# A spectral mixer and an ELU feed-forward layer on one core: the opening's second table as a sum of two short series, other queue orders and PSUM tiles

## The chip, the cores and the metric

The kernel runs on one core of a Trainium2 chip. The core has a matrix engine (TensorE, PE in the profile, its weight loads PEld), a vector engine (VectorE, DVE), a scalar engine (ScalarE, ACT), a general engine (GpSimd, POOL), a queue engine for transfers (SyncE, SP) and 16 DMA engines. Every engine works through its own instructions in order and waits on the others by semaphores. The metric is the device time of one execution in microseconds (us), as a median of several runs.

## The reference

```python
X = np.fft.rfft(x, axis=1)                      # x: (8, 3008, 256)
Xr, Xi = X.real, X.imag
Yr = Xr @ w_r - Xi @ w_i + b_r                  # w_r, w_i: 256 x 256
Yi = Xr @ w_i + Xi @ w_r + b_i
Yr = np.sign(Yr) * np.maximum(np.abs(Yr) - 0.01, 0.0)
Yi = np.sign(Yi) * np.maximum(np.abs(Yi) - 0.01, 0.0)
y = np.fft.irfft(Yr + 1j * Yi, n=3008, axis=1)
h = y.reshape(24064, 256) @ w_in                # w_in: 256 x 2048
g = np.where(h > 0, h, np.exp(np.minimum(h, 0)) - 1)
return g @ w_out                                # w_out: 2048 x 256
```

## The kernel before

The transform over 3008 = 47 x 64 points is done as matmuls with tables of sines: stage A along the 64 (table M1, six units of four rows each), stage X along the 47 with twiddle factors (table M2, eight units), stage M with the weight matrices and the soft threshold (six pairs of groups), stage B back along the 64 (table M3, six units), stage Y back along the 47 (table M4). Between A and X, and between B and Y, the data change their layout by a trip through DRAM: A is stored to DA and read back as Z, B is stored to DB and read back as Bs. The feed-forward layer takes blocks of 512 tokens and pairs of 128 hidden columns: `front` (L790) multiplies by w_in and takes the exponential, `elu` and `finish_elu` make gT, `back` (L848) multiplies by w_out.

The order on every engine is that of the program text (`manual_schedule`, L86). After the opening a plan mixes the units of the next batch between the pairs. In the opening nothing of the feed-forward runs: batch 0 goes through A, X, M, B and the first two units of Y alone, and the first `front` comes behind them. All that the change touches lies in this opening.

The tables are not inputs; they are computed. GpSimd writes integers with iotas (L405), VectorE makes angles of them, ACT takes the sine. M2 has 32 slots (s) of 2 x 48 columns on 96 partitions and is made in four quarters of eight slots: `points` (L498: integer product modulo 64, an index kv, its half as a sign st), `phases` (L514: index times a factor of the partition, plus a phase, on VectorE or ACT), `wraps` (L529: subtract the nearest integer), `sizes` (L541: absolute value, ACT), `signs` (L535) and `sines` (L545: ACT, into M2). `slot0` (L551) masks slot 0. The third table is v3 (L629), its remainder w3 (L676, L677), its absolute value a3 (L683), and two sines (L690), then two products into M3 (L694, L698).

Transfers of x run on GpSimd's queue (L118), in six pieces of 512 KB for batch 0 (`first_x`) and three of 1 MB for batch 1 (`load_x`), the latter behind `gate` (L664), a copy of one column of Z that keeps GpSimd until that part of Z has landed. Stores of A (L157), loads of the weights w_r, w_i (L588, L589), Z (L166), bias rows (L372, L597), w_in (L648), stores of B (L262) and loads of Bs (L273) run on SyncE's queue. GpSimd turns the weights into the bf16 matrices wcat_r and wcat_s (L590 to L593).

`m_group` (L187) does one group of M: four matmuls of 512 columns, with one more in front for the bias if `biased` (L191: a matrix of ones times bias_p, whose rows 0, 32 and 64 hold three bf16 parts of the bias). `first_M` (L222) calls it biased or not in turn; without, VectorE adds bias_bc (L204). The parts are made by L678 to L687.

`idle_pe(n)` (L363) issues n matmuls of 512 columns whose result nobody reads. PSUM in the opening is three pools: pre2 (two tiles of two banks, used by A, X, B and Y), pre1 (three of one bank, for M) and pre0 (the idle matmuls). `unit_X` (L168) does eight matmuls into one pre2 tile and `evac` (L125) copies it to XT on VectorE (L127) or ACT (L129); units 1, 4 and 7 on VectorE.

## Time and profile before

| | us |
|---|---|
| median of 3 runs (lowest to highest) | 910.41 (909.49 to 911.92) |
| the profiled execution | 909.7 |
| its span | 907.9 |
| PE busy in the span | 885.0 (97%) |
| DVE, ACT, POOL busy | 721.0, 698.9, 313.0 |
| first matmul of A, of X, of M | 5.86, 22.43, 30.03 |
| first matmul of B, of the feed-forward | 35.39, 54.07 |

Span is the time from the first to the last instruction of the profile. The page says for each engine how long it was busy; the chain of waits follows the work that ended last back to the start. A granted clock of 1.00 means that TensorE ran unthrottled. One stretch of the opening, with busy time and number of instructions of PE, PEld, DVE, ACT and POOL, then granted clock, DMA share (the mean busy share of the 16 engines) and GB/s:

```profile
22.40:30.70 8.30, 5.47 (x73) 3.60 (x72) 7.53 (x10) 5.45 (x8) 5.45 (x7) 1.00 1.05 321
```

Costs of single operations in the opening, from the trace: a VectorE tensor_scalar of 96x384 f32 0.35, tensor_tensor 0.55, scalar_tensor_tensor 0.61; an ACT activation of 96x384 0.51; an evacuation of X 0.80 on ACT and 0.96 on VectorE; an evacuation of A 1.01 on ACT; a DMA issue on SyncE about 0.25 to 0.54 and on GpSimd 0.6 to 0.8.

### The profile page before, as it was taken

The numbers are of one execution on the slowest core, as the hardware profiler recorded it, in microseconds if no ns is written. First come the engines' busy times: TensorE is split into PE (matmuls) and PEld (weight loads), VectorE is DVE, ScalarE is ACT, GpSimd is POOL, SyncE is SP. The second block draws the span as 40 slices with busy tenths as digits, with TensorE's granted clock in tenths as the row PEclk, the third lists the DMA queues.
The fourth block names the chain that finished last, engine by engine and source line by source line (L and its number), as shares of the span: only waits on it lengthen the run. The fifth ranks groups of instructions, "written<-read, shape, count | busy, mean of one in ns | idle before, by whom it ended". The sixth has DMA issues, their size and how long they took to land.

```text
span 907.9 us, 17273 instructions
## 1 busy us (share of the span) xinstructions
PE 885.0 (97%) x6665; PEld 653.1 (72%) x6768; DVE 721.0 (79%) x901; ACT 698.9 (77%) x855; POOL 313.0 (34%) x436
## 2 busy tenths in 40 slices
PE   9879999999999999999999999999999999999997
PEld 3457667876678676876678766787667866777775
DVE  8779778887788778887788877888778877778776
ACT  6678778787878788788787888878787877777664
POOL 7700440233331431405404153133332134443664
PEclk9999999999999999999999999999999999999999
DMA  8997025721383215722176031752228111221011
GB/s 270 310 258 233 24 70 174 222 70 48 93 232 117 70 48 155 199 88 93 53 204 186 25 106 58 205 167 80 61 73 229 32 40 47 84 80 48 24 47 47
DMA packets 90623, 106.06 MB, mean 117 GB/s; under 512 B 5270, under 2 KB 81308, under 8 KB 87180
## 3 DMA queue, kind: packets, MB, share of 16 engines
q1 hardware_dynamic: 84284, 77.42, 30.5%
q0 software_dynamic: 5968, 27.26, 9.1%
q8 instruction: 53, 0.87, 0.4%
q10 hardware_dynamic: 288, 0.26, 0.1%
q14 instruction: 30, 0.25, 0.1%
HBM read 55.12 MB, written 49.81 MB: 116 GB/s over the span
## 4 chain that ended last, share of the span: by engine, by line
PE 84%; DVE 5%; ACT 4%; DMA 3%; issue 2%; POOL 0%; SPq 0%; DVEq 0%; ACTq 0%; POOLq 0%
PE ps_o L848 34%; PE hps L790 33%; PE mps L194 9%; PE yps L347 2%; PE bps L246 2%; PE aps L146 2%; PE xps L177 2%; DVE gT L817 1%; ACT Bz L259 1%; ACT Et L804 1%; DMA Bs<-DB 1%; DVE Et L829 1%; DMA Z<-DA 1%; ACT Et L801 1%; DMA DB<-Bz 1%
## 5 line engine op out<-in xcount | busy, mean ns | idle before, releaser
L848 PE MATMUL ps_o<-w_out_r,gT 128*128 128x256 f32 x3008 | 476.9, 301 | 0.2 <-DVE gT L815 0.2
L848 PEld LDWEIGHTS ps_o<-w_out_r,gT 128*128 128x128 f32 x3008 | 403.6, 189 | 49.9 <-DVE osb L859 1.3
L790 PE MATMUL hps<-yT,w_in_s 128*128 128x512 bf16 (+7 forms) x1651 | 382.3, 351 | 6.6 <-ACT Bz L259 1.1
L815 DVE SCALAR_TENSOR_TENSOR gT<-Et,hps 128x512 fp32r<-128x512 f32 (+1 forms) x268 | 220.3, 850 | 74.1 <-POOL Et L827 37.6
L817 DVE SCALAR_TENSOR_TENSOR gT<-hps,Et 128x1024 fp32r<-128x1024 f32 x200 | 244.6, 1223 | 16.2 <-DVE Et L829 0.5
L790 PEld LDWEIGHTS <-w_in_s 128*128 128x128 bf16 x1728 | 141.6, 98 | 129.7 <-issue 22.7
L804 ACT ACTIVATE Et<-hps 128x1024 f32<-128x1024 f32 x200 | 206.1, 1030 | 11.1 <-PE hps L790 4.4
L827 POOL TENSOR_SCALAR Et<-Et 128x512 f32<-128x512 f32 x183 | 109.2, 615 | 219.4 <-ACT Et L799 219.4
L829 DVE TENSOR_SCALAR Et<-Et 128x1024 f32<-128x1024 f32 x200 | 138.6, 693 | 48.0 <-ACT Et L804 39.9
L212 POOL TENSOR_SCALAR clip<-yb 128x512 f32<-128x512 f32 x84 | 51.8, 616 | 318.1 <-DVE yb L204 286.0
L799 ACT ACTIVATE Et<-hps 128x512 f32<-128x512 f32 x184 | 99.9, 595 | 62.8 <-PE hps L790 62.1
L801 ACT ACTIVATE Et<-hps 128x1024 f32<-128x1024 f32 x84 | 86.2, 1027 | 71.8 <-PE hps L790 70.2
L213 POOL TENSOR_TENSOR Y<-yb,clip 128x512 bf16<-128x512 f32 x84 | 107.3, 1277 | 7.0
L802 ACT ACTIVATE Et<-Et 128x1024 f32<-128x1024 f32 x84 | 88.9, 1058 | 2.7
L204 DVE TENSOR_TENSOR yb<-mps,bias_bc 128x512 f32<-128x512 f32 x89 | 61.3, 689 | 35.5 <-PE mps L194 23.2
L129 ACT CAST XT<-xps 128x768 bf16<-128x768 f32 x61 | 48.8, 799 | 15.4 <-PE xps L177 15.4
L129 ACT CAST yT<-yps 128x752 bf16<-128x752 f32 (+1 forms) x64 | 49.8, 779 | 13.4 <-PE yps L347 13.2
L129 ACT CAST A<-aps 128x1024 bf16<-128x1024 f32 (+1 forms) x47 | 47.2, 1004 | 13.2 <-PE aps L146 11.6
L194 PE MATMUL mps<-wcat_r,XT 128*128 128x512 bf16 x180 | 55.6, 384 | 0.8 <-ACT Bz L259 0.3
L194 PE MATMUL mps<-wcat_s,XT 128*128 128x512 bf16 x182 | 54.9, 379 | 0.7
L194 PEld LDWEIGHTS <-XT 128*128 128x128 bf16 x384 | 30.8, 98 | 29.6 <-DVE XT L127 0.6
L259 ACT CAST Bz<-bps 128x1024 bf16<-128x1024 f32 x46 | 46.1, 1001 | 2.8 <-PE bps L246 2.8
(121 smaller groups left out, 414.3 us busy)
## 6 DMA issues: line engine op xcount, KB each, us to landing
xt<-in_x_dram POOLq DMA_DIRECT2D x21, 1024.0 KB, 7.5
out_dram<-osb SPq DMA_DIRECT2D x158, 128.0 KB
Bs<-DB SPq DMA_DIRECT2D x31, 384.0 KB
DA<-A SPq DMA_DIRECT2D x21, 512.0 KB
DB<-Bz SPq DMA_DIRECT2D x21, 512.0 KB
Z<-DA SPq DMA_DIRECT2D x7, 1152.0 KB
Z<-DA SPq DMA_DIRECT2D x11, 384.0 KB
xt<-in_x_dram POOLq DMA_DIRECT2D x6, 512.0 KB, 5.8
```

Source lines behind the costliest of these rows:

```text
L129: nc.scalar.copy(dst, src)
L194: nc.tensor.matmul(ps, lhsT=XT[:, dt, c, o : o + P], rhs=wm[:, dt, :], start=(not biased and m == 0 and dt == 0), stop=(m == 1 and dt == 1),)
L213: nc.gpsimd.tensor_tensor(Y_of[b, q][:, i, :], yb, clip[:], ALU.subtract)
L790: nc.tensor.matmul(hps[:, s, c0:c1], lhsT=w_in_s[:, dt, ft * P : ft * P + P], rhs=yT_of[b][:, dt, t0 : t0 + c1 - c0], start=(dt == 0), sto ...
L799: nc.scalar.activation(E_[:, s], hps[:, s], AF.Exp)
L801: nc.scalar.activation(E_, hps[:], AF.Relu, scale=-1.0)
L804: nc.scalar.activation(E_, hps[:], AF.Exp)
L815: nc.vector.scalar_tensor_tensor(o, e, -1.0, h, ALU.add, ALU.max)
L817: nc.vector.scalar_tensor_tensor(o, h, 0.0, e, ALU.max, ALU.add)
L827: eng.tensor_scalar(E_[:, s], E_[:, s], 1.0, 0.0, ALU.min, ALU.max)
L829: nc.vector.tensor_scalar(E_, E_, 1.0, -1.0, ALU.min, ALU.add)
L848: nc.tensor.matmul(po[q][:, i_ % 2, :], lhsT=gT[:, s, i_ * P : i_ * P + P], rhs=w_out_r[:, ft, :], start=(ft == 0 and i_ % 2 == 0), stop=( ...
```

## The change

The index of M2's angle is a product modulo the length; the new text writes the angle as a sum of a term in s alone (`sp`, 32 columns) and a term that depends on a difference only (`tab`, 78 columns), of which `window` takes overlapping, also reversed, pieces without copying; `tsg` holds the sign in the same form. `short_tables` makes them, `sums` adds them in two halves of 16 slots, `wraps` is one instruction that also turns the sign, which the sine's scale takes back. Two columns (n47, sp32) are added; the integer arrays mi, kv, st, r2 and their iotas are dropped.

The first piece of x is loaded ahead of all iotas; ten idle matmuls instead of nine stand at the start and 30 instead of 40 before X. The sixth unit of A is evacuated in halves, one on ACT and one on VectorE, with a store each. On SyncE's queue the loads of Z come ahead of w_r and w_i. The bias is loaded as 8 rows of 64, split into parts on VectorE (`split_bias`), stored to DRAM (bias_d) and loaded back into rows 0, 32 and 64 of bias_p, which GpSimd clears. In X there are three PSUM tiles of two banks, VectorE evacuates units 1, 2, 4, 5 and 7, the third table's work is moved ahead of and into X, and wcat_r, wcat_s are made behind it by VectorE, ACT and GpSimd. The pools pre2 and pre1 are opened behind X. The four matmuls of the first M group are ordered by dt first. The gate of batch 1's loads reads slot 24 of Z.

```diff
-    pre2 = first.enter_context(tc.tile_pool(name="pre2", bufs=2, space=bass.MemoryType.PSUM))
-    pre1 = first.enter_context(tc.tile_pool(name="pre1", bufs=3, space=bass.MemoryType.PSUM))
     pre0 = first.enter_context(tc.tile_pool(name="pre0", bufs=1, space=bass.MemoryType.PSUM))
+    sooner = ExitStack()
+    pre2 = sooner.enter_context(tc.tile_pool(name="preX", bufs=3, space=bass.MemoryType.PSUM))
...
+        j0 = 8 * ci
+        if alone and u == 5:
+            for j in range(2):
+                c = 4 * uu + 2 * j
+                evac(A[:, c : c + 2, :].rearrange("p n d -> p (n d)"), ps[:, j, :], bool(j))
+                nc.sync.dma_start(dav[:, j0 + c : j0 + c + 2, :], A[:, c : c + 2, :])
+            return
...
-        for m, (c, wm) in enumerate(((0, wcat_r), (1, wcat_s))):
-            for dt in range(2):
-                nc.tensor.matmul(
-                    ps, lhsT=XT[:, dt, c, o : o + P], rhs=wm[:, dt, :],
-                    start=(not biased and m == 0 and dt == 0), stop=(m == 1 and dt == 1),
-                )
+        for n_ in range(4):
+            c, dt = (n_ % 2, n_ // 2) if (b, q, i) == (0, 3, 0) else (n_ // 2, n_ % 2)
+            nc.tensor.matmul(
+                ps, lhsT=XT[:, dt, c, o : o + P], rhs=(wcat_r, wcat_s)[c][:, dt, :],
+                start=(not biased and n_ == 0), stop=n_ == 3,
+            )
...
-    brow, rest = (wk3.tile([P, 2 * D], F32, name="yb", tag="yb") for _ in range(2))
-    nc.vector.memset(brow[:], 0.0)
-    for o, bv in ((0, b_r), (D, b_i)):
-        for k in range(3):
...
-    idle_pe(9)
+    BR, BC = 8, 2 * D // 8
+    brow, rest = (wk3.tile([BR, BC], F32, name="yb", tag="yb") for _ in range(2))
+    bpart = wk3.tile([BR, 3, BC], BF16, name="yb", tag="yb")
+    bias_d = dram.tile([3, BR, BC], BF16, name="bias_d", tag="bias_d")
     xts = []
...
+    def first_x(u):
+        load_x(0, u // 2, 4 * (u % 2), 4 * (u % 2) + 4)
+    first_x(0)
+    idle_pe(10)
+    def split_bias():
+        nc.vector.tensor_copy(bpart[:, 0], brow[:])
+        nc.vector.tensor_tensor(rest[:], brow[:], bpart[:, 0], ALU.subtract)
+        nc.vector.tensor_copy(bpart[:, 1], rest[:])
+        nc.vector.tensor_tensor(rest[:], rest[:], bpart[:, 1], ALU.subtract)
+        nc.vector.tensor_copy(bpart[:, 2], rest[:])
...
+        w_r_f = stagep.tile([P, 2, D], F32, name="w_r_f")
+        w_i_f = stagep.tile([P, 2, D], F32, name="w_i_f")
+        for o, bv in ((0, b_r), (BR // 2, b_i)):
+            nc.sync.dma_start(
+                brow[o : o + BR // 2, :],
+                bass.AP(tensor=bv.tensor, offset=bv.offset, ap=[[BC, BR // 2], [1, BC]]),
+            )
...
-        first_x(0)
         first_x(1)
-        mi = stagep.tile([P, NS, K1, 2], I32, name="mi")
-        kk1 = row("kk1", [P, K1, 2])
-        iota("", None, [[1, K1]], out=kk1[:, :, 0])
-        iota("", None, [[-1, K1]], out=kk1[:, :, 1])
         first_x(2)
-        for s0, s1 in ((0, 8), (8, NS)):
...
-                first_x(4)
+        TD, TL = N2 - NS // 2 + K1 // 4, N2 + K1 // 2 + 2
+        trow = iota("trow", [P, TL], [[1, TL]], base=-TD)
+        tji = stagep.tile([P, TL], I32, name="tji")
+        iota("", None, [[-15, TL]], base=15 * TD + 6 * N2, out=tji[:])
+        first_x(3)
+        first_x(4)
+        first_x(5)
+        nc.gpsimd.memset(bias_p[:], 0.0)
...
+        n47 = mix(dve, n1c, 4.0 / N1, qd, ALU.mult, ALU.mult)
+        sp32 = mix(dve, n1s, float(NS), qd, ALU.mult, ALU.add)
...
+        tab = row("tab", [P, TL])
+        tmp = row("tmp", [P, TL])
+        tsg = row("tsg", [P, TL])
+        sp = row("sp", [P, NS])
+        z = slice(0, RZ)
+        def window(t, s0, ns, c, b):
+            return bass.AP(
+                tensor=t.tensor, offset=t[0:RZ, TD - s0 : TD - s0 + 1].offset,
+                ap=[t[0:RZ].ap[0], [-1, ns], [1 - 2 * c, K1]],
+            )
+        def short_tables():
+            dve.tensor_scalar(tmp[:], trow, 36.0 / N1, CMAGIC, ALU.mult, ALU.add)
+            dve.tensor_scalar(tmp[:], tmp[:], -CMAGIC, -float(N1), ALU.add, ALU.mult)
+            dve.scalar_tensor_tensor(tmp[:], trow, 36.0, tmp[:], ALU.mult, ALU.add)
+            dve.tensor_scalar(tmp[:], tmp[:], n47[:], None, ALU.mult)
+            dve.tensor_scalar(tab[:], tmp[:], CMAGIC, -CMAGIC, ALU.add, ALU.add)
+            dve.tensor_tensor(tab[:], tmp[:], tab[:], ALU.subtract)
+            dve.tensor_scalar(sp[:], srow[:, 0:NS], n1s[:], ph[:], ALU.mult, ALU.add)
+            dve.tensor_scalar(tji[:], tji[:], N2 - 1, None, ALU.bitwise_and)
+            dve.tensor_scalar(tsg[:], tji[:], NS + 0.5, -0.5, ALU.is_gt, ALU.add)
+        def kt(t, s0, s1):
+            return t[z, s0:s1].rearrange("p s (k t) -> p s k t", t=2)
+        def sums(s0, s1):
+            for c in range(2):
+                dve.tensor_tensor(
+                    kt(v2, s0, s1)[:, :, :, c],
+                    sp[z, s0:s1].unsqueeze(2).to_broadcast([RZ, s1 - s0, K1]),
+                    window(tab, s0, s1 - s0, c, None), ALU.add,
+                )
+            if s0 == 0:
+                dve.tensor_scalar(
+                    kt(v2, 0, 1)[:, 0, :, 1], tab[z, TD - NS : TD - NS + K1], sp32[z], None,
+                    ALU.add,
+                )
+        def wraps(s0, s1):
+            v = v2[z, s0:s1]
+            dve.scalar_tensor_tensor(v, v, 0.5, v, ALU.is_gt, ALU.subtract)
+        def sizes(s0, s1):
+            nc.scalar.activation(a2[z, s0:s1], v2[z, s0:s1], AF.Abs)
+        def signs(s0, s1):
+            for c in range(2):
+                a = kt(a2, s0, s1)[:, :, :, c]
                 dve.scalar_tensor_tensor(
-                    kv[z, 0, :, 1], mi[z, 0, :, 1], float(N1), kk1[z, :, 0], ALU.mult, ALU.add
+                    a, a, qd[z], window(tsg, s0, s1 - s0, c, None), ALU.subtract, ALU.mult
                 )
-            kf = k_.rearrange("p s k t -> p s (k t)")
...
-        def wraps(g):
-            gs, z = slice(8 * g, 8 * g + 8), slice(0, RZ)
-            v, r = v2[z, gs], r2[z]
-            dve.tensor_scalar(r, v, CMAGIC, -CMAGIC, ALU.add, ALU.add)
-            dve.tensor_tensor(v, v, r, ALU.subtract)
...
+        def sines(s0, s1, c):
             nc.scalar.activation(
-                M2[:, gs, c, :], (v2, a2)[c][z, gs], AF.Sin, bias=0.0, scale=TURN * (1.0 + c)
+                M2[:, s0:s1, c, :], (v2, a2)[c][z, s0:s1], AF.Sin, bias=0.0,
+                scale=(-TURN, 2.0 * TURN)[c],
             )
...
-            unit_A(0, u, alone=True)
+            unit_A(0, u, alone=True, on_dve=False)
...
-        points(0)
-        phases(0)
-        wraps(0)
-        for u in range(4):
+        short_tables()
+        sums(0, 16)
+        wraps(0, 16)
+        sums(16, 32)
+        wraps(16, 32)
+        for u in range(6):
             fA(u)
-        points(1)
-        phases(1, True)
-        points(2)
-        sizes(0)
-        fA(4)
-        wraps(1)
-        signs(0)
-        fA(5)
+            if u == 2:
+                sizes(0, 16)
+                signs(0, 16)
+        for g in range(4):
+            load_Z(0, 8 * g, 8 * g + 8)
         nc.sync.dma_start(w_r_f[:], w_r.rearrange("(c p) e -> p c e", p=P))
         nc.sync.dma_start(w_i_f[:], w_i.rearrange("(c p) e -> p c e", p=P))
-        pool.tensor_copy(wcat_r[:, :, 0:D], w_r_f[:])
-        pool.tensor_copy(wcat_r[:, :, D : 2 * D], w_i_f[:])
-        pool.tensor_scalar(wcat_s[:, :, 0:D], w_i_f[:], -1.0, None, ALU.mult)
-        pool.tensor_copy(wcat_s[:, :, D : 2 * D], w_r_f[:])
-        for g in range(4):
-            load_Z(0, 8 * g, 8 * g + 8)
+        sizes(16, 32)
+        signs(16, 32)
+        sines(0, 16, 0)
+        sines(0, 16, 1)
+        slot0()
+        sines(16, 32, 0)
+        sines(16, 32, 1)
+        split_bias()
+        nc.sync.dma_start(bias_d.rearrange("k r c -> r k c"), bpart[:])
         for o, bv in ((0, b_r), (D, b_i)):
             nc.sync.dma_start(
                 bias_bc[:, o : o + D],
                 bass.AP(tensor=bv.tensor, offset=bv.offset, ap=[[0, P], [1, D]]),
             )
-        sines(0, 0)
-        sizes(1)
-        phases(2, True)
+        for k in range(3):
+            nc.sync.dma_start(
+                bias_p[32 * k : 32 * k + 1, :], bias_d[k : k + 1].rearrange("k r c -> k (r c)")
+            )
         dve.tensor_scalar(m3i[:], m3i[:], 63, None, ALU.bitwise_and)
         k3 = row("k3", [P, NV])
         dve.scalar_tensor_tensor(k3[:], m3i[:], float(N1), k1t[:], ALU.mult, ALU.add)
         dve.tensor_scalar(sg3[:], k3[:], S // 2 + 0.5, -0.5, ALU.is_gt, ALU.add)
-        points(3)
-        phases(3)
-        wraps(2)
-        signs(1)
-        sines(0, 1)
-        sines(1, 0)
-        sizes(2)
-        sines(1, 1)
-        wraps(3)
-        signs(2)
-        slot0()
-        sines(2, 0)
-        sizes(3)
-        sines(2, 1)
-        signs(3)
-        sines(3, 0)
-        sines(3, 1)
         full = [P, NV, N2]
         k3b = k3[:].unsqueeze(2).to_broadcast(full)
         dve.scalar_tensor_tensor(
             v3[:], n2row.unsqueeze(1).to_broadcast(full), 1.0 / S, k3b, ALU.mult, ALU.mult
         )
-        idle_pe(40)
+        dve.tensor_scalar(w3[:], v3[:], CMAGIC, -CMAGIC, ALU.add, ALU.add)
+        dve.tensor_tensor(w3[:], v3[:], w3[:], ALU.subtract)
+        def sin3(k):
+            o, src, sc, bi = ((1, w3, TURN, 0.0), (0, a3, -TURN, hpi[:]))[k]
+            nc.scalar.activation(
+                M3[:, :, 0, o * N2 : o * N2 + N2], src[:], AF.Sin, bias=bi, scale=sc
+            )
+        idle_pe(30)
+        for u in range(8):
+            unit_X(0, u, alone=True, on_dve=u not in (0, 3, 6))
+            if u == 0:
+                nc.scalar.activation(a3[:], w3[:], AF.Abs)
+            if u == 3:
+                sin3(0)
+            idle_pe(1)
+        dve.tensor_copy(wcat_r[:, :, 0:D], w_r_f[:])
+        nc.scalar.activation(wcat_s[:, :, 0:D], w_i_f[:], AF.Copy, scale=-1.0)
+        dve.tensor_copy(wcat_r[:, :, D : 2 * D], w_i_f[:])
...
-    gate(Z_of[0][:, 8, 0:1])
+    gate(Z_of[0][:, 24, 0:1])
...
-    nc.vector.tensor_scalar(w3[:], v3[:], CMAGIC, -CMAGIC, ALU.add, ALU.add)
-    nc.vector.tensor_tensor(w3[:], v3[:], w3[:], ALU.subtract)
-    nc.scalar.copy(bias_p[:], brow[:])
-    nc.vector.tensor_tensor(rest[:], brow[:], bias_p[:], ALU.subtract)
-    for u in range(8):
-        unit_X(0, u, alone=True, on_dve=u in (1, 4, 7))
-        if u == 1:
-            nc.scalar.activation(a3[:], w3[:], AF.Abs)
-            nc.vector.tensor_copy(bias_p[32:64], rest[32:64])
-            nc.vector.tensor_copy(bias_p[64:P], rest[64:P])
-            nc.vector.tensor_tensor(rest[64:P], rest[64:P], bias_p[64:P], ALU.subtract)
-            nc.vector.tensor_copy(bias_p[64:P], rest[64:P])
-        idle_pe(1)
-    for o, src, sc, bi in ((1, w3, TURN, 0.0), (0, a3, -TURN, hpi[:])):
-        nc.scalar.activation(
-            M3[:, :, 0, o * N2 : o * N2 + N2], src[:], AF.Sin, bias=bi, scale=sc
-        )
+    sooner.close()
+    pre2 = first.enter_context(
+        tc.tile_pool(name="pre2", bufs=2, space=bass.MemoryType.PSUM, reuse_waits="tile")
+    )
+    pre1 = first.enter_context(
+        tc.tile_pool(name="pre1", bufs=3, space=bass.MemoryType.PSUM, reuse_waits="tile")
+    )
```

## The prediction

> **What bounds the kernel now.** I read the page first (span 907.9 us, 909.7 us with what lies around it, 0.7 us under the median 910.41), and there the 40 slices: TensorE is at nine tenths from the fifth slice to the last but one. All that the diff touches runs before 54 us, so the question is how many microseconds the opening loses, and whether the rest simply starts that much sooner. Then I read the chain of waits in order of time:
>
> ```profile
> 1.47 4.26 DMA xt<-in_x_dram
> ...
> 11.10 1.01 ACT A L129
> 12.11 0.61 ACT v L518
> ...
> 23.85 1.10 DVE yb L679
> 24.95 0.88 DVE XT L127
> 25.82 0.04 issue
> 25.87 0.51 PE xps L177 x8
> ...
> 29.74 0.97 DVE XT L127
> 30.71 0.05 issue
> 30.75 0.82 PE mps L194 x3
> ```
>
> A transfer starts it; then ACT mixes evacuations of A with angles (L518 between two of them); then VectorE, up to a bias split (L679) that holds an evacuation of X; from 30.75 it is TensorE's matmuls of M. One matmul of M(3,0) began earlier, at 30.03, and waited; with 0.215 us each, M(3,0) has done what it would have done by starting at 30.75 - 0.215 = 30.54 us. **30.54 is the mark** against which I set the new start of M.
>
> Next the timeline of SyncE's queue, which shows when the transfers between the stages are issued:
>
> ```profile
> 8.13 7.25 SPq L157 DMA_DIRECT2D DA<-A  x6
> 15.43 0.54 SPq L588 DMA_DIRECT2D w_r_f<-in_w_r_dram  x1
> 16.02 0.49 SPq L589 DMA_DIRECT2D w_i_f<-in_w_i_dram  x1
> 18.21 1.74 SPq L166 DMA_DIRECT2D Z<-DA  x4
> ...
> 45.66 0.32 SPq L273 DMA_DIRECT2D Bs<-DB  x1
> ```
>
> The sixth store of A is issued at 15.02 (15.38 less one issue of 0.36); Z waits for its landing until 18.21, so 3.2 us, and both weight loads lie in between. The stretches say how full the DMA engines are (the last three columns are granted clock, DMA share and GB/s):
>
> ```profile
> 4.00:13.00 9.00, 8.49 (x29) 3.19 (x27) 7.68 (x27) 4.97 (x7) 8.06 (x26) 1.00 1.08 363
> 13.00:18.50 5.50, 5.26 (x24) 2.47 (x25) 5.19 (x15) 5.31 (x11) 1.69 (x3) 1.00 1.06 318
> 18.50:26.00 7.50, 5.84 (x49) 3.25 (x49) 7.40 (x13) 5.14 (x9) 7.19 (x7) 1.00 0.94 238
> 26.00:40.50 14.50, 13.17 (x99) 6.29 (x99) 10.31 (x16) 9.23 (x13) 9.50 (x11) 1.00 1.21 378
> ```
>
> Full from 4 to 18.5 us: three resources (DMA, VectorE, ACT) are each nearly the bound of the opening.
>
> **The change, part by part.**
>
> *First load of x ahead of the iotas.* GpSimd issues it at 0.84 instead of 1.47 (where pcol stands now), 0.63 us sooner. pcol, srow and qrow move behind one issue of 0.73, but VectorE loses the clear of brow (0.48 at 1.45), so M1 is not later. The six pieces land now at 5.8, 7.0, 8.7, 10.2, 11.7 and 13.1 (issue plus time to landing), 1.3 to 1.7 apart: bandwidth. The gain on the last is between 0 (the second piece is issued no sooner) and 0.63; I take 0.4: 12.7. The tenth idle matmul (0.43 each here, the array being cold) keeps unit 0 from starting before 5.7, which costs nothing while unit 5 waits for data.
>
> *Second table.* VectorE now spends per quarter of M2 0.35 + 0.55 + 0.36 on points, 0.46 on phases (or ACT 0.70), 0.36 + 0.55 on wraps and 0.61 on signs. New: nine operations of 78 columns (nearest row 128x64, 0.21 to 0.28 with its start: 2.3), two columns more (0.3), sums 4 x 0.55 plus one of 0.2, two wraps of 768 elements (0.95 each, from the 128x768 of L629), signs 4 x 0.62. From the end of M1 at about 4.4 this makes, with the seven columns that stay (1.1), the first wrap done at 10 to 10.5, the second at 12.2 to 12.7 and signs of the first half at 13.4 to 14. ACT loses both phases (1.4), and takes sizes(0,16) (0.9) between A units 2 and 3.
>
> *Last A unit in halves, and the queue order.* Unit 4 is evacuated on ACT until about 13.2; then ACT's half takes 0.59 and VectorE's, behind the signs, 0.69: stores issued by 13.8 to 14.6, against 15.02. The landing took 3.2 us with the two loads beside it (2 x 256 KB, which at 318 GB/s are 1.6 us of DMA time). Without them it is between 2.0 and 3.2. Byte count as a cross-check: x and A were 4.7 MB, moved by 17.0 as the engines ran; started 0.4 sooner, 16.6. I take Z's issue at **16.7**, 1.5 us sooner (bounds 16.2 to 17.7).
>
> *X.* The fourth Z piece is bounded by bytes: after 18.5 the 1.57 MB of Z and 0.26 MB of bias_bc moved at 238 GB/s until 26, so Z's last byte came at about 25.4 and was usable by 26 at the latest; I take 7.6 us after the issue, so 24.3 (bounds 23.5 to 25.5). After it come two units of X (0.55 each and an idle matmul of 0.21: 1.35), an evacuation on VectorE (0.96) and two copies into wcat_r there (0.42 each, from L684; 0.70 in L687 is the upper bound). 24.3 + 1.35 + 0.96 + 0.84 = 27.45. VectorE's own sum, 14.2 after the A half, then signs 1.27, a wait for ACT's sines to 16.7, slot0 0.9 to 1.4, the split 1.0, k3 0.5, the third table 0.94 + 0.6 to 0.85 + 0.96, five evacuations 4.8 and the copies 0.84, ends at 27.2 to 28.1. The two agree within a microsecond; the upper ends of slot0 and L676 were taken while GpSimd cast the weights (L590 to L593, 18.75 to 24.4), work that is gone from there, so I take M at **27.3** (bounds 26.2 to 28.9). The third PSUM tile removes the 1.55 us that TensorE waited before 25.87; without it that stall, now of evacuations u1 and u2 behind the third table, would return. 30 idle matmuls instead of 40 end at about 13.5 + 30 x 0.213 = 19.9; that costs nothing as long as Z is not there. ACT's third-table sines and the scaled weight copy (0.84 + 0.85 + 0.60 + 0.92) fit between its three evacuations; the last sine ends near 28 and is needed by the first B, five groups later.
>
> *The weights* now land behind Z: 0.52 MB at 238 to 318 GB/s is 1.6 to 2.2 us more, so about 26.2, just ahead of the copies at 26.5: nothing, if so; each microsecond beyond is paid in full.
>
> *The bias parts.* Removed from VectorE behind X: 1.10 + 0.42 + 0.42 + 0.69 + 0.70 = 3.3 us, and 0.60 on ACT; added five operations of 64 columns ahead of X (counted). But the parts now go to DRAM and back, a store and three loads in SyncE's queue. Behind the store's wait stand bias_bc, the three loads, load_w_in(0) and the first DB stores. The store is issued at about 19.8; if it lands at once (3.2 us) the loads are there by 26, if it moves after Z and the weights (26.3) they are issued at 27 and land at 28.5 to 29.5. The first biased group, M(3,1), wants them at 27.3 + 0.9 = 28.2. I charge 0.1 (0 to 1.3).
>
> A rule bears on this. The Trainium skill (DMA: Bandwidth & Descriptors, "Queues, rings and completion order") says that on each engine the descriptors of one queue are consumed in ring order. By it the late end of the store holds, and the sum would be about 0.7 worse; the rows agree as far as they go (weights issued behind the last A store landed behind it, at 18.7).
>
> *Gate on Z's slot 24 instead of 8, and behind the weight buffers.* x(1) and w_out(0) are issued from about 28 instead of 24.98; they took until 40.4 (26.90 + 13.5), so now until 43.5. First user of x(1) is at 47.9 less the gain, of w_out at 59.6: nothing. What they meet is below.
>
> **Sum.** 30.54 - 27.3 - 0.1 = 3.1: 909.7 - 3.1 = 906.6 for an execution like the profiled one, **907.3** as a median. From 30.75 to 54 the chain is matmuls of M and their evacuations, which moves as a block.
>
> **Rivals.** 0.3% of the time, 2.7 us, is about what a measurement of this kernel tells from no change.
>
> (a) *As summed*, 907.3, own range 906.0 to 908.6: **0.60**. With Z at its lower bound M starts at 26.2: 906.2 as a median.
>
> (b) *Z is not sooner.* VectorE's signs run late, the half is stored at 14.6 and lands 3.2 later: Z at 17.7, M at 28.6, gain 1.9; with a bias stall of 0.6, 1.3: 909.1. For it: VectorE's 5.19 of 5.50 busy, and a first operation of 1.15 instead of 0.35 (L502). **0.20**.
>
> (c) *TensorE falls to half clock.* It has nothing between 19.9 and Z's first piece (20.7). Trace: a wait of 1.55 us left X's matmuls at 0.20 us. The Trainium skill (TensorE: Matmul & The Clock Gate, "Why this matters for your kernels") warns of gaps over about 3 us. A gap that long needs Z at 23. X and M then run at half speed as the first matmuls do (0.43): some 8 groups of 0.86, limited to about 4 us of it, 2 lost: 909.3. **0.05**.
>
> (d) *The other side: the bias trip meets the x(1) stream.* Place: PE's in-order queue at M(3,1). If the store lands only at 27 and the three loads then queue against the 4 MB issued from 25 to 28 on GpSimd, they take what a loaded round trip takes (DB store 42.26 to Bs landed 48.46: 6.2): 33.2, against 28.2 wanted: 5.0 lost, of which the 3.2 gained before it pay the most: net 1.8 slower, 912.2. It decides from a landing of 31.4 on, and by 0.3% from 34.1 on. Against: the gate holds x(1) until the weights are copied. The same stream can delay Bs, wanted 2.2 us after it landed: it begins to cost when the round trip exceeds 8.4. **0.15**, more than half of it beyond 0.3%, as both delays may meet.
>
> Faster by over 0.3% means under 907.7: three quarters of (a) and a quarter of (b), 0.45 + 0.05, and a little for gains that I have left out, 0.52. Slower is 0.10, from (d). The rest, 0.38, is the same. The range runs from Z's lower bound, with half a microsecond of scatter and one for what is uncosted (904.9), over (b) and (c) into the near part of (d) (911.0).
>
> **What would show it.** Right: Z issued near 16.7; the chain in the opening made of DMA, then VectorE (XT L127, wcat_r), then M from 27.3; no wait of X on PSUM; the first B near 32.3 instead of 35.39; the first front at 51.0 instead of 54.07. Wrong: the chain passing through bias_p or w_i_f (d), Z at or after 17.5 (b), matmuls of X at 0.4 (c), POOL's gate on Bs later than 48.5, or a front that starts 3.1 sooner and an end that does not.

## The result and the profile after

| | median, us (lowest to highest) | runs |
|---|---|---|
| before | 910.50 (909.49 to 911.95) | 6 |
| after | 916.06 (913.51 to 917.35) | 6 |

The ratio is 1.0055 (95%: 1.0039 to 1.0071): the changed kernel is slower by 5.6 us, where 3.1 us sooner was forecast. The profiled execution took 916.46 us with a span of 914.7, so 6.8 us more span than the 907.9 before. The table follows the opening from mark to mark.

| us | before | forecast | after |
|---|---|---|---|
| Z's first load issued | 18.21 | 16.7 | 18.38 |
| M in motion (before: the mark) | 30.54 | 27.3 | 30.74 |
| x(1) issued | 24.98 | about 28 | 31.45 |
| first B | 35.39 | 32.3 | 36.31 |
| GpSimd's gate on Bs | 48.48 | not later | 54.66 |
| first feed-forward front | 54.07 | 51.0 | 58.26 |
| first Y matmul behind the opening's two Y units (yps) | 63.57 | | 69.47 |
| end of the span | 907.9 | | 914.7 |

Up to M nothing is gained and 0.2 lost; between M and 69.47 another 5.7 us go. From there on the loss grows only from 5.9 to 6.8. The chain of waits of the changed kernel, in order of time (start, duration, what):

```profile
5.13 8.88 DMA xt<-in_x_dram
...
14.88 0.59 ACT A L129
15.48 0.02 issue
15.50 0.70 DVE A L127
16.20 0.02 issue
16.22 2.14 DMA DA<-A
...
19.69 8.12 DMA Z<-DA
...
30.81 0.05 POOL gate L685
...
34.99 1.28 POOL Y L239
36.27 0.04 issue
36.31 0.63 PE bps L252 x8
...
38.43 10.54 DMA w_in_f<-in_moe_w_in_dram
48.97 0.02 issue
48.99 0.43 DVE w_in_s L678
...
58.24 6.70 DMA DB<-Bz
...
65.02 4.41 DMA Bs<-DB
69.42 0.05 issue
69.47 0.51 PE yps L353 x8
```

Before, the path left the opening through VectorE and then ran on TensorE. Now it runs through the last Z piece (8.12 us of its trip) and then through four things more: a gate on GpSimd at 30.81, GpSimd's part of the first B group, one weight transfer of 10.54 us (w_in(1)), and the trip through DRAM of B, 6.70 for the store and 4.41 for the load (before, the same store was issued at 54.04 and the load behind it at 58.15, and Y did not wait for it). None of these four stood on the path that I worked with.

SyncE's queue shows the order of the issues (start, issue time summed over the group):

```profile
15.50 1.09 SPq L155 DMA_DIRECT2D DA<-A  x2
18.38 1.73 SPq L172 DMA_DIRECT2D Z<-DA  x4
20.16 0.61 SPq L603 DMA_DIRECT2D w_r_f<-in_w_r_dram  x1
20.81 0.50 SPq L604 DMA_DIRECT2D w_i_f<-in_w_i_dram  x1
21.35 0.40 SPq L613 DMA_DIRECT2D bias_d<-yb  x1
...
29.28 0.83 SPq L620 DMA_DIRECT2D bias_p<-bias_d  x3
30.15 0.40 SPq L668 DMA_DIRECT2D w_in_f<-in_moe_w_in_dram  x1
...
51.78 0.32 SPq L279 DMA_DIRECT2D Bs<-DB  x1
```

The queue stands from 22.9 to 29.28 for the landing of the 3 KB store of the bias parts, and w_in(0), issued at 24.43 before, stands behind it until 30.15. On GpSimd, meanwhile:

```profile
30.81 0.70 POOL L685 CAST gate<-Z 96x1 f32<-96x1 bf16 x1 [1.84 <-ACT M L636]
31.45 1.90 POOL L118 DMA_DIRECT2D xt<-in_x_dram  x3
33.13 1.12 POOL L673 DMA_DIRECT2D w_out_r<-in_moe_w_out_dram  x1
34.07 0.84 POOL L238 TENSOR_SCALAR clip<-yb 128x512 f32<-128x512 f32 x1
```

The gate had more to wait for than Z's slot 24. Its tile lies in a pool that is opened when the opening's stage closes, so it stands behind the readers of that stage, and the change puts X and, behind X, the weight copies inside it. The profile puts the wait down to ACT's sine (L636), which ended at 30.55; VectorE's copy of w_i_f (L650) ended at 30.60, and in a_w_first the profile names that copy. The trace cannot tell the two apart, but of these only the copy reads a buffer of the stage, and in the five profiles with this gate the gate starts 0.21 to 0.22 us behind the copy. x(1) is issued 6.5 us later than before, and the four issues push GpSimd's first clip from 32.40 to 34.07; TensorE's first B then waits 0.66 us for GpSimd's Y. With both queues held at once the DMA engines run empty. Two stretches of the changed kernel (busy time of PE, PEld, DVE, ACT, POOL; then granted clock, DMA share, GB/s):

```profile
28.50:31.00 2.50, 0.91 (x12) 0.49 (x11) 2.13 (x5) 2.06 (x3) 0.66 (x2) 1.00 0.03 9
52.00:55.00 3.00, 2.85 (x24) 1.98 (x23) 1.91 (x3) 1.37 (x3) 0.17 (x1) 0.56 0.70 168
```

And the same two of the kernel before:

```profile
28.50:31.00 2.50, 1.92 (x21) 1.06 (x21) 1.85 (x3) 1.91 (x4) 0.00 (x0) 1.00 1.04 403
52.00:55.00 3.00, 1.54 (x13) 0.97 (x13) 2.38 (x5) 1.29 (x2) 0.00 (x0) 1.00 1.13 324
```

In the first stretch 403 GB/s have become 9: 1 MB less moved, and all that comes behind it stands later. What that does some 18 us later, in the timeline of the changed kernel:

```profile
48.99 0.43 DVE L678 TENSOR_SCALAR w_in_s<-w_in_f 128x512 bf16<-128x512 f32 x1 [2.36 <-DMA w_in_f<-in_moe_w_in_dram]
50.27 0.29 PE L316 MATMUL tps<-M,Y 64*128 64x32 bf16 x8 [2.46 <-DVE yb L329]
```

w_in(1) is issued at 38.43, 0.9 us later than before, but lands 10.5 us after it, behind the late x(1) and w_out(0). VectorE's scaling of it (45.31 before) waits in order, the yb evacuation waits behind it, and TensorE stands 2.46 us. Then the granted clock drops: 0.56 in the second stretch. The front that began at 54.07 now begins at 58.26.

The DMA engines over the window from 18 to 31 us of the changed kernel (40 slices of 0.325 us: busy tenths, GB/s, and what was moved) tell of the second loss, that of the 3.1 us:

```profile
DMA  0000778869997997989999899999999610000000
GB/s 2 0 0 0 63 164 214 214 265 391 340 340 202 265 277 265 315 252 239 290 277 268 202 233 202 255 240 299 321 363 302 205 49 22 13 0 0 3 3 3
DMA packets 1322, 2.39 MB, mean 184 GB/s; under 512 B 164, under 2 KB 936, under 8 KB 1320
```

They are empty until 19.3 (the landing of A's last store has nothing beside it any more) and then move Z, both weights and bias_bc, 2.39 MB, as one batch that ends at 28.1. The last Z piece is usable at 27.8, at the end of the batch.

### The profile page after: what moved, and what is told of

The parts are those of the page before. It is cut to its first block, busy times and chain, and to the rows that moved or that the text cites. A ratio compares the mean times of both kernels' runs of the same rounds, so it can differ in the third digit from the quotient of the medians.

```text
span 914.7 us, 17335 instructions
## 1 busy us (share of the span) xinstructions
PE 889.7 (97%) x6759; PEld 653.0 (71%) x6759; DVE 716.8 (78%) x899; ACT 694.6 (76%) x845; POOL 306.0 (33%) x429
## 4 chain that ended last, share of the span: by engine, by line
PE 84%; DMA 6%; ACT 3%; DVE 3%; issue 2%; POOL 1%; SPq 0%; DVEq 0%; ACTq 0%; POOLq 0%
PE ps_o L858 34%; PE hps L800 33%; PE mps L200 8%; PE yps L353 2%; PE bps L252 2%; PE xps L183 2%; PE aps L146 2%; DMA Bs<-DB 1%; DMA DB<-Bz 1%; DMA w_in_f<-in_moe_w_in_dram 1%; ACT Bz L265 1%; DVE gT L827 1%; DMA xt<-in_x_dram 1%; DMA Z<-DA 1%; DVE Et L839 1%
## 5 line engine op out<-in xcount | busy, mean ns | idle before, releaser
L800 PE MATMUL hps<-yT,w_in_s 128*128 128x512 bf16 (+4 forms) x1728 | 389.0, 353 | 2.3 <-ACT Bz L265 1.1
L827 DVE SCALAR_TENSOR_TENSOR gT<-hps,Et 128x1024 fp32r<-128x1024 f32 x200 | 244.6, 1223 | 16.2 <-PE hps L800 0.5
L200 PE MATMUL mps<-wcat_r,XT 128*128 128x512 bf16 x192 | 58.2, 384 | 1.9 <-DVE wcat_r L650 1.6
L129 ACT CAST A<-aps 128x1024 bf16<-128x1024 f32 (+1 forms) x47 | 46.8, 996 | 16.2 <-PE aps L146 12.5
L200 PE MATMUL mps<-wcat_s,XT 128*128 128x512 bf16 x192 | 57.3, 379 | 0.0
```

Of the source, the lines that this page charges most:

```text
L129: nc.scalar.copy(dst, src)
L200: nc.tensor.matmul(ps, lhsT=XT[:, dt, c, o : o + P], rhs=(wcat_r, wcat_s)[c][:, dt, :], start=(not biased and n_ == 0), stop=n_ == 3,)
L800: nc.tensor.matmul(hps[:, s, c0:c1], lhsT=w_in_s[:, dt, ft * P : ft * P + P], rhs=yT_of[b][:, dt, t0 : t0 + c1 - c0], start=(dt == 0), sto ...
L827: nc.vector.scalar_tensor_tensor(o, h, 0.0, e, ALU.max, ALU.add)
```

## The experiments

Each ratio is against runs of the kernel before on the same chip. M is the first matmul of M, the front the first matmul of the feed-forward, both in the profiled execution. In three kernels (before, b_x1_late, b_bias) the second matmul of M waits, so that M's mark is 30.54, 30.70 and 29.91.

| | median, us | before | ratio (95%) | x(1) issued | M | front |
|---|---|---|---|---|---|---|
| before | | 910.50 | | 24.98 | 30.03 | 54.07 |
| the change | 916.06 | 910.50 | 1.0055 (1.0039 to 1.0071) | 31.45 | 30.74 | 58.26 |
| b_x1_late | 914.44 | 910.12 | 1.0044 (1.0029 to 1.0059) | 31.86 | 30.19 | 57.81 |
| x1_early | 916.38 | 910.12 | 1.0067 (1.0052 to 1.0082) | 28.48 | 31.78 | 58.68 |
| x1_w0_early | 915.71 | 910.12 | 1.0066 (1.0046 to 1.0086) | 28.96 | 32.26 | 60.70 |
| x1_early_warm | 914.68 | 910.18 | 1.0053 (1.0039 to 1.0066) | 28.98 | 32.28 | 57.50 |
| x1_bias_warm | 912.89 | 910.59 | 1.0032 (1.0020 to 1.0043) | 28.67 | 31.97 | 55.28 |
| a_one_A | 914.31 | 910.12 | 1.0045 (1.0030 to 1.0060) | 31.88 | 31.17 | 59.44 |
| a_w_first | 915.00 | 910.53 | 1.0057 (1.0039 to 1.0075) | 33.75 | 33.04 | 58.49 |
| a_warm | 914.94 | 910.53 | 1.0058 (1.0040 to 1.0075) | 31.98 | 31.27 | 57.44 |
| a_scale_late | 915.90 | 910.53 | 1.0064 (1.0048 to 1.0079) | 31.26 | 30.55 | 57.97 |
| c_best1 | 911.02 | 910.53 | 1.0006 (0.9996 to 1.0015) | 26.71 | 30.75 | 54.26 |
| c_best2 | 910.07 | 910.18 | 0.9995 (0.9986 to 1.0004) | 25.82 | 30.75 | 54.24 |
| b_bias | 908.91 | 910.18 | 0.9987 (0.9978 to 0.9997) | 24.84 | 29.40 | 52.26 |
| b_bias_psum3 | 909.34 | 910.59 | 0.9989 (0.9980 to 0.9998) | 25.50 | 30.24 | 53.75 |

**x(1) late, alone.** In the kernel before, the gate is put on X's last column, behind X; nothing else is changed.

```
-    gate(Z_of[0][:, 8, 0:1])
-    for ci in range(3):
-        load_x(1, ci)
-    load_w_out(0)
...
+    gate(XT_of[0][:, 1, 0, 24:25])
+    for ci in range(3):
+        load_x(1, ci)
+    load_w_out(0)
```

> The kernel before with one edit: gate, x(1) and w_out(0) stand behind X and read its last column, so they are issued from about 31.4 instead of 25.0, as in the changed kernel; w_in(0) stays at 24.4. S: 913 to 916 us, w_in(1) or Bs late. O: 911.5 or less, since M starts where it did.

914.44, 4.3 us slower than before, with M all but unmoved (30.19). Three lines of its timeline of TensorE show where (start, busy, instruction, idle time before it and what ended it):

```profile
36.71 0.61 PE L246 MATMUL bps<-Y,M 64*128 64x256 bf16 x8 [1.09 <-POOL Y L233]
49.86 0.29 PE L310 MATMUL tps<-M,Y 64*128 64x32 bf16 x8 [1.64 <-DVE yb L323]
57.81 1.02 PE L790 MATMUL hps<-yT,w_in_s 128*128 128x512 bf16 x4 [1.10 <-ACT Bz L259]
```

They are the waits of the changed kernel: the first B on GpSimd's Y, then TensorE behind VectorE, which waited for w_in(1) at 48.58; the clock was 0.50 from 51 to 53.5. x(1) and w_out(0) issued some 7 us later, which the prediction priced at nothing, cost 4.3 us by themselves. Not all of it is the stream: the four issues now stand right ahead of GpSimd's first clip, and the first B comes 1.3 us later than before (36.71 instead of 35.39), of which 0.2 are M's; w_in(1) is issued 1.3 us later behind it. Of the 3.7 us by which the front is late, I estimate from these rows 1.1 for GpSimd and the rest for late transfers and the clock.

**x(1) early, in the changed kernel.** The gate gets a column of its own in the stage's pool and goes, with x(1) and w_out(0), ahead of X and of the weight copies on GpSimd; in x1_w0_early w_in(0) also goes ahead of the three loads of the bias parts, into a buffer of its own.

```
+        gate0 = stagep.tile([P, 1], F32, name="gate0")
+        nc.gpsimd.tensor_copy(gate0[0 : 2 * NR, :], Z_of[0][:, 24, 0:1])
+        for ci in range(3):
+            load_x(1, ci)
...
-    gate(Z_of[0][:, 24, 0:1])
-    for ci in range(3):
-        load_x(1, ci)
-    load_w_out(0)
```

> The changed kernel with one edit: GpSimd's gate uses a column of its own, and gate, x(1) and w_out(0) stand ahead of the weight copies, still behind Z's slot 24. Theory S (streams): the 4 MB are issued from about 28 instead of 31.45, the DMA engines' empty stretch from 28.5 to 31.5 goes, w_in(1) lands by about 46 instead of 48.97 and GpSimd's clips are no longer behind four issues; 911 to 913 us. Rival O (the opening itself is longer, the transfers only follow): 915 us or more.

> As before, and w_in(0) has a buffer of its own and is issued ahead of the three loads of bias_p, so that it waits neither for the bias store's landing nor for the weight buffers. S: both streams are back near their old places, about 910 us, one to two less than with x(1) alone. If the bias trip holds nothing but itself: the same as x(1) alone. O: 915 or more.

Neither gets anything back: 916.38 and 915.71. x(1) is issued 3 us sooner and other waits take its place: M at 31.78 in the first (TensorE waited 2.54 us for wcat_r), then 1.26 us on the bias parts, and the granted clock is 0.50 in x1_early's stretch from 31.5 to 37.5 (in x1_w0_early from 31.2 to 41.5):

```profile
31.50:37.50 6.00, 4.46 (x11) 1.40 (x12) 2.96 (x4) 0.27 (x1) 3.10 (x3) 0.50 1.05 401
```

To take the clock out of it, x1_early_warm adds ten idle matmuls ahead of X and twelve behind it.

```
-        idle_pe(30)
+        idle_pe(40)
...
+    idle_pe(12)
```

> The changed kernel with x(1) and w_out early, as in the run of that name, and idle matmuls that keep TensorE from standing still: 40 instead of 30 ahead of X and 12 behind it. With x(1) alone M waited 2.5 us for the copies and 1.3 for bias_p, and the granted clock was 0.50 from 31.4 to 37.5. If that half clock ate what the early streams gave (8 us at half speed, some 4 us of work): clock 1.00 there, the feed-forward from 54 to 55.5 instead of 58.68, 911 to 913 us. If the streams never were the loss: 915 or more.

The clock stays at 1.00 until 57.2 us (then 0.50 for 3.4 us), and 914.68 remain. The bias parts now show as they were foreseen in rival (d), in the timelines of SyncE's queue and of TensorE:

```profile
29.86 0.83 SPq L620 DMA_DIRECT2D bias_p<-bias_d  x3
35.21 0.38 PE L197 MATMUL mps<-bias_p,busy 128*128 128x512 bf16 x1 [1.75 <-DMA bias_p<-bias_d]
```

Three loads of 1 KB, the last issued at 30.4, are usable at 35.1, beside the 4 MB of x(1) and w_out(0). In the changed kernel, where the engines were all but idle then, the same loads, issued from 29.28, were not waited for at 31.60.

**Bias parts early as well.** x1_bias_warm moves the split ahead of A's units, its store behind A's fourth unit, and the three loads right behind Z.

```
+        split_bias()
         for u in range(6):
             fA(u)
+            if u == 3:
+                nc.sync.dma_start(bias_d.rearrange("k r c -> r k c"), bpart[:])
```

> The changed kernel with both remedies and the idle matmuls: x(1) and w_out early, and the bias split ahead of A, stored behind A's fourth unit and loaded back right behind Z. In the run without the second remedy x(1) was early, but bias_p landed at 35.07, 4.6 us after its issue beside x(1), and M(3,1) began at 35.2 instead of 31.6. If the loss was the one or the other, whichever the order put behind: M(3,1) by 33.2, the feed-forward at 55 to 56, 911 to 912.5 us. If something else in the changed opening costs the 4 to 5 us: 914 or more.

912.89, 2.3 us over its before of 910.59, where the change stood 5.6 over its own: with the stream early, the bias parts in time and the clock up, 3.3 us are back. No wait on the bias parts is left. What remains is M at 31.97, and the timeline of VectorE shows what delays it:

```profile
30.11 0.47 DVE L656 CAST wcat_r<-w_r_f 128x512 bf16<-128x512 f32 x1
30.50 1.32 DVE L658 CAST wcat_r<-w_i_f 128x512 bf16<-128x512 f32 x1
```

The weight copies still follow X on VectorE, and the second takes 1.32 us instead of 0.42, while GpSimd issues w_out(0) (30.35 to 31.6): it ends at 31.82, and the idle matmuls put there end at 31.97.

**Single parts of the change undone.** a_one_A evacuates the sixth unit of A whole, on ACT. a_w_first puts the two weight loads ahead of Z again. a_warm puts eleven idle matmuls where TensorE stood at 47.8. a_scale_late moves half of w_in(1)'s scaling behind the work that waited for it.

```
-        if alone and u == 5:
-            for j in range(2):
...
```
```
-        for g in range(4):
-            load_Z(0, 8 * g, 8 * g + 8)
         nc.sync.dma_start(w_r_f[:], w_r.rearrange("(c p) e -> p c e", p=P))
         nc.sync.dma_start(w_i_f[:], w_i.rearrange("(c p) e -> p c e", p=P))
+        for g in range(4):
+            load_Z(0, 8 * g, 8 * g + 8)
```
```
+    idle_pe(11)
     turn_B(2)
```
```
-    scale_w_in(1, True, 0)
     first_M(2, 1, True)
...
     store(True)
+    scale_w_in(1, True, 0)
```

> The changed kernel with the sixth A unit evacuated whole on ACT with one store. In the changed kernel the VectorE half began only when ACT's half had ended (14.88 to 15.47, 15.50 to 16.19). If the two halves exclude each other whatever engine they are on: the store is issued at about 15.9, not later than the second half's 16.2, Z within 0.5 us of 18.38, and the time the same within 1.5 us. If halving gains as predicted: Z 0.5 to 1 us later and the time as much longer.

> The changed kernel with w_r and w_i loaded ahead of Z again. By the step of the prediction on the last store of A, Z is issued 0.5 to 1.2 us later than 18.38. If the weights behind Z took Z's bandwidth, as the fourth piece landing 9.4 us after the issue says, that piece still lands by about 27.8 and the copies into wcat_r no longer wait: M at or before 30.7. If rings are strictly in order, Z's last piece lands as much later as the issue, and M with it, 31.3 or later.

> The changed kernel with 11 idle matmuls ahead of turn_B(2), where TensorE stood still for 2.5 us until VectorE had w_in(1), and after which its granted clock was 0.50 from 52 to 55.6. Theory C (the stall is paid twice, once as a wait and once as half clock behind it): the clock stays at 1.00, the wait stays, the first matmul of the feed-forward comes 1 to 1.7 us sooner than 58.26, and the time is 914.5 to 915. If the clock has no part: the same 916, or longer by the idle work.

> The changed kernel with the first half of the scaling of w_in's second quarter moved behind the second B unit, beside its other half, so that VectorE isn't held by it. Theory S, narrowed: late w_in(1), blocking VectorE's queue, costs about 2.4 us and the clock behind it 1.4: feed-forward from 54.5 to 55.5 instead of 58.26, 911.5 to 913.5 us. If the DB to Bs trip in the same backlog sets the end anyway: the feed-forward starts sooner, but the units of Y still wait for Bs near 69.4, and the time falls by less than 1.5.

All four lie between 914.3 and 915.9, and their intervals overlap that of the change: undoing any one of them alone brings little or nothing back. Their times do not price the parts, because TensorE's half clock falls elsewhere in each (a_one_A from 49.9 to 56.7, a_w_first from 23.4 to 30.2 and from 57.5 to 64.3, a_warm from 24.5 to 27.9, a_scale_late from 30.3 to 33.7 and from 54.2 to 61.0). Their traces say more. In a_one_A x came later (unit 5's matmuls at 14.75 instead of 14.14), but counted from there Z is issued 4.27 us behind, against 4.24 with the halves: the halves gain nothing. In a_w_first Z is issued at 18.24, no later than with the weights behind it: the landing of A's last store does not depend on them. In a_warm the clock is 1.00 from 50 to 56 and the front comes 0.8 us sooner (1.35 counted from M, which came 0.5 later there). In a_scale_late VectorE's wait for w_in(1) is gone, but TensorE waits 2.2 us for Bs ahead of Y (54.01), and the front comes only 0.3 us sooner. So with one late transfer out of the way the next one is the limit. a_w_first pays at another place: with the weights first, Z reaches X later (23.77 instead of 22.49), X runs at half clock, and M starts at 33.04.

**The parts put together otherwise.** c_best1 keeps the tables, the three PSUM tiles and the shares of X; it issues x in the old order, evacuates A whole, loads the weights ahead of Z and copies them on GpSimd and ACT ahead of X, sends the bias parts early, and has x(1) behind Z's slot 16. c_best2, of which the lines below are, also puts the gate on slot 8, X behind the stage of the tables, w_in(0) in its old buffer, and 42 idle matmuls.

```
+        pool.tensor_copy(wcat_r[:, :, 0:D], w_r_f[:])
+        pool.tensor_copy(wcat_r[:, :, D : 2 * D], w_i_f[:])
         nc.scalar.activation(wcat_s[:, :, 0:D], w_i_f[:], AF.Copy, scale=-1.0)
...
+    gate(Z_of[0][:, 8, 0:1])
```

> Of the change only the short tables, the third PSUM tile and X's shares of the engines are kept; x in the old order, A whole on ACT, weights ahead of Z and cast on GpSimd and ACT as they land, the bias parts split ahead of A and back from DRAM ahead of X, w_in(0) in a buffer of its own, x(1) behind slot 16 of Z. If the tables and X's part are sound and the streams were the loss: M at 28 to 29, no stretch of empty DMA before 36, 908 to 909.5 us. If the opening is bound by the bytes alone: M at 30 or later, 910 or more.

> As the first combined kernel, with X behind the table stage as in the kernel before, so that w_in(0), the gate (slot 8 again) and x(1) wait for the casts alone and not for X, w_in(0) in its old buffer and behind Z's bandwidth, and 42 idle matmuls. If TensorE's half clock in X (0.50 from 25 to 28.8 there) and w_in(0) beside Z held it at 911.0: M at 29 to 29.7, x(1) at 24 to 25, 908.5 to 909.8 us. If the opening is bound by the bytes ahead of Z's landing: M at 30 or later, 910 to 911.

911.02 and 910.07: neither can be told from the kernel before. The second table as two short series and the third PSUM tile, in this company, bring nothing that can be measured. That they cost nothing is not shown: both kernels also have the bias parts early, which alone gain 1.3 us (b_bias, below), so the rest may cost about as much. The loss of the change lies in the orders that these two kernels take back (x, the last A unit, weights and their copies, bias parts, gate).

**The bias parts alone, in the kernel before.** b_bias puts the parts' DRAM trip into the kernel before, with the split and the store early and the loads behind Z. b_bias_psum3 adds the third PSUM tile.

```
+        split_bias()
         for u in range(4):
             fA(u)
+        nc.sync.dma_start(bias_d.rearrange("k r c -> r k c"), bpart[:])
...
-    nc.scalar.copy(bias_p[:], brow[:])
-    nc.vector.tensor_tensor(rest[:], brow[:], bias_p[:], ALU.subtract)
```

> The kernel before with the bias part of the change alone, put early: 8 rows of 64 are split on VectorE ahead of A, stored behind A's fourth unit and loaded back behind Z. It takes 3.3 us of VectorE and 0.6 of ACT out of X, where L679 held an evacuation for 1.5 us. If VectorE sets X there: M at 28.8 to 29.8 instead of 30.54, 909 to 909.8 us. If Z's landing sets it: M at 30 or later and no difference, within 0.5 us.

> The kernel before with the early bias parts, which ran at 908.9, and the change's three PSUM tiles for X. There TensorE still waited 1.1 us for a tile in X. If that wait sets X: M 0.5 to 1.1 us sooner than 29.40, 908 to 908.7 us. If Z's landing or the last evacuation sets it: the same within 0.4 us.

b_bias is the fastest of all: 908.91 (11 runs), 0.9987 (0.9978 to 0.9997) of the kernel before, with the first M matmul at 29.40 and the front at 52.26. Of the 1.8 us by which this front is sooner M explains 0.6; in this one profile the front also goes without the wait of 1.10 us for ACT's evacuation of B that stands ahead of it before, and why is not known. Two stretches show DMA full and TensorE busy throughout the second:

```profile
28.50:31.00 2.50, 2.06 (x17) 0.90 (x14) 1.83 (x3) 2.36 (x3) 0.00 (x0) 1.00 1.06 414
31.00:40.50 9.50, 9.50 (x61) 4.11 (x59) 6.09 (x10) 5.93 (x9) 8.12 (x8) 1.00 1.28 390
```

With the third PSUM tile it is 909.34, 0.9989 (0.9980 to 0.9998): the same. In that profile X waits 1.4 us for Z, and no longer for PSUM.

## Why the prediction was wrong, step by step

**The step that failed** is "Gate on Z's slot 24 instead of 8, and behind the weight buffers": x(1) and w_out(0) "from about 28 instead of 24.98 ... nothing". I asked only when the first user of x(1) and of w_out would want them. The price is with what stands behind them: w_in(1), DB and Bs share the engines with these 4 MB, and GpSimd's first clip stands behind the four issues. 6.9 us of delay came back as 4.3 us of time in b_x1_late, which has nothing else of the change. The date was off too (31.45 instead of 28), and for the same reason as M: the weight copies that the gate stands behind were planned to end at 27.3 and ended at 30.60. I had noted "What they meet is below" and then followed just the bias trip and the first Bs; w_in(1), scaled in order on VectorE, was left out. My cover that "the chain is matmuls of M and their evacuations, which moves as a block" fell with it: the block meets transfers that do not move with it.

**M at 27.3** failed as well, by 3.4 us (30.74), so the gain that should have paid for the rest was not there. Z's last piece was usable at 27.8 instead of 24.3; of these 3.5 us 1.7 are its later issue and 1.8 its longer trip. By the terms:
- *Last x piece at 12.7*: unit 5's first matmul began at 14.14, 0.9 later than before. GpSimd's first issue went out at 1.25 and its second at 2.63 (before 1.47 and 2.20). In nine profiles with the new order unit 5 began at 13.90 to 14.75; in six with the old one at 13.24 to 13.82, but for one at 14.66. That the order is the cause is likely, but argued, not isolated.
- *Halves stored by 13.8 to 14.6*: they did not run side by side. ACT 14.88 to 15.47, then VectorE 15.50 to 16.19, which the timeline puts down to a wait for ACT's A. The last store left at about 16.2, 1.2 later than before, and a_one_A, without halves, loses nothing against it when counted from unit 5's start.
- *Landing 2.0 to 3.2*: 2.14. The size was right, and the reason was not: with the weights ahead, a_w_first issued Z just as early.
- *Z's last piece 7.6 after its issue*: 9.4 (18.38 to 27.8). The weights were meant to land "behind Z ... nothing, if so". The batch of 2.39 MB finished as one at 28.1. Before, the weights had moved while the landing of A's last store was awaited; the share from 13 to 18.5 us was 1.06, and is now 0.88. That the weights behind Z stretched its trip is not shown: with the weights ahead the last piece was usable 9.5 us after the issue in b_bias_psum3 (18.49 to 28.0) and 9.6 in c_best2 (18.93 to 28.5). The 7.6 itself was too small; it came from a profile in which X never waited for the last piece.
- *Copies into wcat_r, 0.84 behind X*: as costed (29.85 to 30.60), and on the path, as forecast; they are late because Z is.

Two sums of the prediction are off by little and change nothing: two units of X and an idle matmul are 1.31, not 1.35, and 906.2 less 0.5 and 1 is 904.7, not 904.9.

The Trainium skill (DMA: Bandwidth & Descriptors, "Queues, rings and completion order") says that descriptors of one queue are consumed in ring order on each engine, and that completion is still not first in, first out per issuing engine. The bias store, issued last but for bias_bc, landed at 29.2, at the end of the batch, as by that rule; the last Z piece, issued ahead of 0.79 MB, was no more than 0.3 us from the batch's end, so being issued first did not let it land early here.

**Rival (d)** is a real mechanism, under a condition that the change itself avoids: only when x(1) is early do the loads of the bias parts meet its stream (usable at 35.1, TensorE waits 1.75 us). In the changed kernel the parts came before x(1), no wait on bias_p stands in the chain, and the slow side was reached by the opposite route, with x(1) late. But the trip's other effect, which I had listed among the things standing behind the store ("load_w_in(0)"), was not priced: w_in(0) came 5.7 us later. **Rival (c)**, 0.05, named the wrong place: X kept its full clock, and the half clock came at 52 us. The bound was taken too high, and it is not a bound on the length of a gap. The Trainium skill (TensorE: Matmul & The Clock Gate, "Why this matters for your kernels") warns of gaps over about 3 us; here 0.50 came with standstills of 1.62, 1.64, 2.03, 2.46 and 2.54 us (a_warm, b_x1_late, c_best1, the change, x1_early), but also where the longest near it was 1.59 (a_scale_late at 30.3) or 1.10 (x1_early_warm at 57.2, a_w_first at 57.5), and a wait of 1.75 (x1_early_warm at 35.2) left 1.00. What the traces show in its place is at the end. Its own share is small: a_warm removes the one at 52 us and moves the front by 0.8, 1.35 counted from M.

**What was right**: the bias split was worth removing from behind X (b_bias gains 1.3 us, with M 0.6 sooner); the second table and its company cost at most about what the early bias parts gain (c_best2 against b_bias); X no longer waits for PSUM, but Z takes its place as the limit, so the tile is worth nothing measurable (b_bias_psum3 against b_bias).

**What stays open**: how the 5.6 us divide. Late x(1) and w_out(0) alone are 4.3, putting three things right brings back 3.3, and the shares overlap, since each removed wait uncovers the next; and the 2.3 us that x1_bias_warm still loses were not split between x and the weight copies. Why two halves of one tile on two engines run one after the other was not tried apart.

## What to carry to other kernels

A transfer that is put off is not priced by its own first user but by every transfer behind it on the same engines: look for stretches where the DMA share was full and would now be empty, and count the bytes that then come late, and look at what the issuing engine has to do next. A gate costs what its own buffer waits for, too: here it stood behind the weight copies, and every microsecond by which these came late was passed on to 4 MB of loads. And the order of the issues in one queue is not the order of landing: Z, issued first, was usable at the end of the batch, 9.4 us after its issue with the weights behind it and 9.5 to 9.6 with the weights ahead.

## What the runs showed of the hardware

- The granted clock of TensorE changes in steps of 3.41 us. The 14 stretches of half clock that ten of the traces show between 6 and 90 us last 3.4, 6.8 or 10.2 us, and where a trace has two, their edges lie whole multiples of 3.41 apart. In the 3.41 us ahead of each drop TensorE was busy for 0.35 to 0.52 of the time; no step of this grid with a larger share was followed by a drop, and three steps of 0.49 to 0.52 were not either. So no single gap decides: a drop came during or behind several short waits as well as behind one of 2.5 us, and in some cases before work was taken up again. In a_w_first it took nearly the whole of X:

```profile
23.50:30.00 6.50, 6.01 (x53) 4.72 (x55) 2.92 (x4) 3.08 (x4) 0.00 (x0) 0.50 0.64 146
```

- Small transfers pay the whole queue: 3 KB of bias parts took 7.9 us to DRAM (21.35 to 29.2) behind the Z batch, and 1 KB loads took 4.6 us beside x(1).
- A VectorE cast of 128x512 took 1.32 us beside a GpSimd DMA issue and 0.42 without one.
